# State in head rows, an early second batch, loads issued one by one, and 64-column tiles in a cross-attention and mixer kernel

## The chip, the core and the metric

The kernel runs on one core of one Trainium2 chip. The metric is device time in microseconds (us). Executions of one kernel mostly agree within a per cent or so. Each execution carries a state: "slow" here means over 1.5% above the fastest of the same kernel. A ratio is the mean time of one kernel's fast runs over that of the kernel before in the same rounds on the same chip, so it is not quite the ratio of the medians that stand beside it. Ratios come with a 95% interval.

## The reference

There are 8 batches and 8 heads. `x` has 512 tokens of 64 columns per head, `state` has 32. Both parts attend to each other; the joined 544 tokens of 512 columns then go through a mixer.

```python
scores  = scale * x @ state^T            # per batch and head: 512 x 32
xread   = softmax(scores)  @ state       # 512 x 64
scores2 = scale * state @ x^T            # 32 x 512
sread   = softmax(scores2) @ x           # 32 x 64
y = concat(xread, sread) on tokens, heads joined on columns     # 8 x 544 x 512
W_tok = scale * (y @ w_q) @ (y @ w_k)^T  # 544 x 544
out   = relu(W_tok @ y) @ w_out          # 8 x 544 x 512, float32
```

## The kernel before

The whole program is one list of tokens, `name.batch.engine`, and each token emits one step. The engine letter is `p` for POOL, `v` for DVE, `a` for ACT, `t` for TensorE. So the list fixes the order on every engine. Steps that matter here: `ixN` loads batch N of `x`; `stc` casts the state to bfloat16, `stt` transposes it, `ste` and `stf` evict it; `stbd` builds block-diagonal state; `xT` transposes `x`; `pt` and `exp` are scores; `A` normalises on POOL; `wq`, `wk`, `v`, `mix` and `fin` are the mixer.

```python
    st_f = const.tile([B * H, NS, D], FP, name="st_f")     # state: 64 rows (batch, head)
    nc.sync.dma_start(out=st_f, in_=state...)              # 512 KB, the first load of all
    for g in range(4):                                     # batch 0 of x, in float32
        eng = nc.sync if g % 2 == 0 else nc.scalar
        eng.dma_start(out=x_f0[:, 2 * g : 2 * g + 2], in_=xsrc(0, 2 * g, 2 * g + 2))
    ...
    def load(n, b, e):                                     # batches 1 to 7 and w_out:
        if n == "iwo":                                     # POOL's queue casts to bfloat16
            nc.gpsimd.dma_start(out=w_o, in_=moe_w_out.rearrange("(k p) e -> p k e", p=128))
        else:
            b = int(n[2:])
            nc.gpsimd.dma_start(out=x_bf[b], in_=xsrc(b, 0, H))
    ...
    def st_back(n, b, e):        # the transposed state is transposed back into head rows
    ...
```

In the list of before all of `ix1` to `ix7` and `iwo` are issued between 8.2 and 18.6 us. They stand in one queue, called the casting queue below.

The softmax here doesn't subtract the row's maximum and nothing guards it: scores larger than these inputs give would overflow.

## Time and profile before

| | before |
|---|---|
| median (range) | 95.72 us (95.07 to 96.07, 4 runs) |
| span of the profiled run | 93.4 us |
| TensorE busy | 85% |
| TensorE's waits for the state | 2.4 + 2.4 us |
| TensorE's last matmul to the end | about 5.6 us |

### The profile page before, as it was taken

What the parts mean: (1) busy time and instruction counts of PE and PEld (TensorE: products, weight loads), DVE (VectorE), ACT (ScalarE), POOL (GpSimd) and SP (SyncE); (2) the same over time, 40 slices, a digit from 0 to 9 for tenths busy, and PEclk for the clock granted to TensorE, in tenths of its full rate; (3) what the DMA queues carried; (4) which work ended last, traced back from release to release, by engine and by line L of the source; (5) the groups of instructions that cost most, each with busy time, mean ns of one, the idle gap of its engine ahead of it and who ended that gap; (6) DMA issues with size and microseconds to landing.
All of it is one profiled execution on the core that took longest, in us unless ns stands there. A gap on an engine that the chain in (4) does not pass through costs nothing.

```text
span 93.4 us, 3134 instructions
## 1 busy us (share of the span) xinstructions
PE 79.8 (85%) x1376; PEld 53.4 (57%) x1376; DVE 56.2 (60%) x109; ACT 53.6 (57%) x80; POOL 44.6 (48%) x58
## 2 busy tenths in 40 slices
PE   5908098998995999999999999999999999999500
PEld 3506086896864676888366547646668644444100
DVE  1026948589584959896496198965786487222500
ACT  2324746687894687359967647864054876444200
POOL 7307994894499989899500009339750000000000
PEclk9998555599999999999999999999999999999985
DMA  1998799999999915500032517806455004428990
GB/s 28 305 260 193 94 160 156 205 203 194 197 199 197 201 18 232 225 11 0 0 130 102 225 22 213 311 30 270 186 225 232 0 0 164 173 39 300 400 363 21
DMA packets 12933, 15.13 MB, mean 162 GB/s; under 512 B 1592, under 2 KB 10296, under 8 KB 12856
## 3 DMA queue, kind: packets, MB, share of 16 engines
q0 software_dynamic: 7808, 4.19, 33.2%
q1 hardware_dynamic: 4280, 9.70, 29.3%
q10 hardware_dynamic: 832, 1.05, 3.8%
q8 instruction: 10, 0.16, 0.7%
q14 instruction: 3, 0.02, 0.1%
HBM read 10.22 MB, written 8.91 MB: 205 GB/s over the span
## 4 chain that ended last, share of the span: by engine, by line
PE 76%; ACT 6%; DMA 6%; DVE 4%; issue 2%; DVEq 0%
PE fin_ps L538 30%; PE xT_ps L246 9%; DMA st_f<-in_state_dram 6%; PE pt_ps L264 5%; PE mix_ps L504 5%; PE at_ps L322 4%; PE srd_ps L335 3%; PE wq_ps L398 3%; PE wk_ps L436 3%; DVE stT L139 3%; ACT xT L137 2%; PE fins_ps L538 2%; PE srd_ps L348 2%; PE v_ps L468 2%; PE g_ps L452 2%
## 5 line engine op out<-in xcount | busy, mean ns | idle before, releaser
L538 PE MATMUL fin_ps<-w_o,rmix 128*128 128x512 bf16 x128 | 30.0, 379 | 0.0
L309 POOL TENSOR_TENSOR A<-E,rinv 128x1024 bf16<-128x1024 bf16 (+1 forms) x9 | 15.3, 1718 | 15.5 <-DVE rinv L303 15.5
L538 PEld LDWEIGHTS <-rmix 128*128 128x128 bf16 x128 | 11.6, 98 | 12.5 <-ACT rmix L143 0.3
L137 ACT COPY ost<-fin_ps 128x1024 f32<-128x1024 f32 (+1 forms) x10 | 9.3, 928 | 14.1 <-PE fin_ps L538 13.6
L139 DVE COPY ost<-fin_ps 128x1024 f32<-128x1024 f32 (+1 forms) x8 | 8.7, 1089 | 11.1 <-PE fin_ps L538 7.5
L280 ACT ACTIVATE E<-pt_ps 128x512 bf16<-128x512 f32 x16 | 9.6, 603 | 4.3 <-PE pt_ps L264 4.3
L372 POOL TENSOR_TENSOR sbd<-srn,mask 128x256 bf16<-128x256 bf16 x16 | 9.5, 612 | 4.4 <-DVE srn L362 4.1
L295 DVE TENSOR_REDUCE rsum<-E 128x16 f32<-128x512 bf16 x16 | 10.6, 672 | 1.1 <-ACT E L280 1.1
L246 PE MATMUL xT_ps<-ident,x_bf 128*128 128x128 bf16 x128 | 11.0, 238 | 0.1
L145 DVE TENSOR_SCALAR rmix<-mix_ps 128x1024 bf16<-128x1024 f32 x7 | 8.5, 1223 | 2.7 <-PE mix_ps L504 2.6
L137 ACT COPY xT<-xT_ps 128x1024 bf16<-128x1024 bf16 x9 | 9.1, 1020 | 1.5 <-PE xT_ps L246 1.5
L143 ACT ACTIVATE rmix<-mix_ps 128x1024 bf16<-128x1024 f32 x9 | 9.3, 1032 | 0.7 <-PE mix_ps L504 0.5
L213 POOL TENSOR_TENSOR stbd<-st_bf,mask 128x256 bf16<-128x256 bf16 x16 | 9.3, 614 | 0.0
L246 PEld LDWEIGHTS <-x_bf 128*128 128x128 bf16 x128 | 8.4, 106 | 1.0 <-issue 0.4
L264 PE MATMUL pt_ps<-stT,xT 128*128 128x64 bf16 x128 | 7.1, 203 | 0.5 <-DVE xT L139 0.4
L504 PE MATMUL mix_ps<-wq,V 64*128 64x256 bf16 x64 | 5.7, 272 | 1.2 <-issue 1.1
L152 POOL DMA_DIRECT2D x_bf<-in_x_dram x7 | 6.6, 944 | 0.0
L264 PEld LDWEIGHTS <-xT 128*128 128x128 bf16 x128 | 5.6, 105 | 1.6 <-DVE xT L139 0.5
L139 DVE COPY xT<-xT_ps 128x1024 bf16<-128x1024 bf16 x7 | 4.8, 686 | 2.2 <-PE xT_ps L246 2.0
L139 DVE COPY AT<-at_ps 128x1024 bf16<-128x1024 bf16 x7 | 4.8, 685 | 1.2 <-PE at_ps L322 1.2
L322 PE MATMUL at_ps<-ident,A 128*128 128x128 bf16 x64 | 5.0, 219 | 0.0
L504 PEld LDWEIGHTS <-V 64*128 64x128 bf16 x64 | 2.4, 94 | 3.8 <-issue 2.8
(76 smaller groups left out, 115.9 us busy)
## 6 DMA issues: line engine op xcount, KB each, us to landing
out_dram<-ost SPq DMA_DIRECT2D x14, 512.0 KB, 3.8
x_bf<-in_x_dram POOLq DMA_DIRECT2D x7, 512.0 KB, 13.4
out_dram<-ost SPq DMA_DIRECT2D x4, 256.0 KB, 2.1
st_f<-in_state_dram SPq DMA_DIRECT2D x1, 512.0 KB, 5.6
x_f<-in_x_dram ACTq DMA_DIRECT2D x2, 256.0 KB, 4.3
x_f<-in_x_dram SPq DMA_DIRECT2D x2, 256.0 KB, 6.3
w_o<-in_moe_w_out_dram POOLq DMA_DIRECT2D x1, 512.0 KB, 10.5
out_dram<-ost ACTq DMA_DIRECT2D x2, 256.0 KB, 3.9
```

Source lines behind the costliest of these rows:

```text
L137: nc.scalar.copy(out=out, in_=in_)
L139: nc.vector.tensor_copy(out=out, in_=in_)
L143: nc.scalar.activation(out=out, in_=in_, func=AF.Relu)
L213: nc.gpsimd.tensor_tensor(out=stbd[:, b, r], in0=st_bf[:, b, r : r + 1, :].to_broadcast((128, NP, D)), in1=mask[:, :, None].to_broadcast(( ...
L246: nc.tensor.transpose(out=ps[:, u, q, :], in_=x_bf[b][:, NP * r + q, 128 * u : 128 * u + 128], identity=ident,)
L264: nc.tensor.matmul(out=ps[:, 2 * u : 2 * u + 2, NS * q : NS * q + NS], lhsT=L[b][f"xTe{r}"][:, u, q, :], rhs=stT[:, b, :, NP * r + q, :], ...
L280: nc.scalar.activation(out=L[b]["E"][:, r].rearrange("p c q n -> p c (q n)"), in_=L[b][f"pt{r}"], func=AF.Exp, scale=float(scale),)
L295: nc.vector.reduce_sum(out=L[b]["rsum"][:, w], in_=L[b]["E"].rearrange("p r c q n -> p (r c q) n")[:, w], axis=AX.X,)
L309: eng.tensor_tensor(out=L[b]["A"].rearrange("p r c q n -> p (r c q) n")[:, w], in0=L[b]["E"].rearrange("p r c q n -> p (r c q) n")[:, w], ...
L372: nc.gpsimd.tensor_tensor(out=L[b]["sbd"][:, r], in0=L[b]["srn"][:, r : r + 1, :].to_broadcast((128, NP, D)), in1=mask[:, :, None].to_broa ...
L504: nc.tensor.matmul(out=ps[:, h, kk, :], lhsT=L[b]["V"][rows, 128 * k : 128 * k + 128], rhs=L[b]["wq"][rows, 0:SH], start=True, stop=True,)
L538: nc.tensor.matmul(out=ps, lhsT=lhs(k), rhs=w_o[:, k, :], start=(k == 0), stop=(k == KC - 1))
```

## The change

The intent is an earlier start and no state wait: load the state in the rows in which it is wanted, in three pieces (batch 0; 1 and 2; 3 to 7), with the last piece held back; issue `x1` early and `x4` to `x7` late, so that they don't crowd the queue; fill the early gaps with dummy matmuls that keep the clock up; and split some matmuls into two 64-column tiles.

```diff
-    st_f = const.tile([B * H, NS, D], FP, name="st_f")
+    st_f = const.tile([128, B, 2, D], FP, name="st_f")
+    gate = st_f[:, 3, 0, 0:1]
+    st_src = state.rearrange("b (r q) n d -> (q n) (b r) d", r=2)
+    def st_load(b0, b1):
+        nc.sync.dma_start(out=st_f[:, b0:b1], in_=st_src[:, 2 * b0 : 2 * b1])
+    st_load(0, 1)
     ... x0 in four loads
+    st_load(1, 3)
...
+    def fill(n, b, e):                         # b dummy matmuls of 512 columns
...
+    def mm(m, out, lhsT, rhs, **kw):
+        if m == "c":                           # two 64-column tiles
...
+    def st_gate(n, b, e):
+        nc.gpsimd.memset(gate, 0.0)            # the load below must wait for this write
+        st_load(3, B)                          # batches 3 to 7, 320 KB
...
-    def st_back / stb_ev                       # way back of the state: gone
...
+        if e == "b":                           # last output tile: half on DVE, half on ACT
```

In the list (cut):

```diff
-zst.0.p stc0.0.v ... ix1.0.p ... ix2.0.p ... iwo.0.p ... ix3.0.p ... ix4.0.p ... ix5.0.p ... ix6.0.p ... ix7.0.p
+zst.0.p ix1.0.p stc.0.v fill.1.t stt.0.c ... ix2.0.p ... fill.10.t ... iwo.0.p ... stbd.1.p ... stg.0.p
+... ix3.0.p ... stc.2.v ... v.0.c ... ix4.0.p ... fin3.0.c ix5.0.p ... xTe0.5.v ix6.0.p ... xT0.6.t ix7.0.p
```

## The prediction

> **What bounds the kernel now.** I read the page first (busy shares, then the 40 slices), then TensorE's waits, then the chain of work that ended last, and last a table of busy time per microsecond for the start. From the page, busy time and share by engine, then the slices:
>
> ```profile
> PE 79.8 (85%) x1376; PEld 53.4 (57%) x1376; DVE 56.2 (60%) x109; ACT 53.6 (57%) x80; POOL 44.6 (48%) x58
> ...
> PE   5908098998995999999999999999999999999500
> ...
> PEclk9998555599999999999999999999999999999985
> ```
>
> A slice is 93.4/40 = 2.33 us. TensorE is full from slice 8 (about 19 us) to slice 37, so the long middle is bound by TensorE's own stream. The losses are in front: holes in slices 0 to 12, and a half clock in slices 4 to 7. TensorE's waits, longest first:
>
> ```profile
> PE stT_ps L180 <- DVE st_in L139: 2.4, 1, 2.4
> PE stb_ps L201 <- ACT stT L137: 2.4, 1, 2.4
> PE mix_ps L504 <- issue: 1.1, 1, 1.1
> PE warm_ps L127 <- DVE mask L128: 1.1, 1, 1.1
> ```
>
> The two waits of 2.4 us are both about the state: first for its 512 KB load (issue to landing 5.6 us) and cast, then for four evictions of the transposed state, one after another. Per microsecond (busy time and count on PE, PEld, DVE, ACT, POOL, then granted clock, DMA share, GB/s):
>
> ```profile
> 8.00:9.00 1.00, 0.96 (x26) 0.68 (x20) 1.00 (x1) 0.00 (x0) 1.00 (x2) 0.82 0.82 138
> 9.00:10.00 1.00, 0.09 (x1) 0.00 (x0) 0.97 (x2) 0.86 (x1) 1.00 (x2) 0.50 0.08 18
> ...
> 18.00:19.00 1.00, 1.00 (x18) 1.00 (x16) 0.46 (x1) 0.33 (x1) 1.00 (x2) 0.56 1.24 208
> ```
>
> So the clock fell to half near 8.7 us and came back near 18.9. The chain (start, length, what) gives TensorE's prices:
>
> ```profile
> 39.36 0.34 PE v_ps L468 x2
> 39.69 0.22 PE v_ps L477 x4
> 39.91 0.22 PE v_ps L468 x2
> 40.13 0.22 PE v_ps L477 x4
> 40.35 0.22 PE wq_ps L398 x4
> ...
> 51.67 1.73 PE fin_ps L538 x8
> ...
> 72.65 1.09 ACT V L490 x2
> 73.74 0.01 issue
> 73.75 1.03 ACT rmix L143
> ...
> 87.77 0.59 ACT ost L137
> ```
>
> Eight 512-column matmuls take 1.73 us, 0.216 each. Two 512-column matmuls on 64-column tiles take 0.22 together, so they run side by side. The same pair right after full-array work costs 0.34. I compared all pieces of the chain after 20 us with columns/2.4 GHz plus 2.5 ns: the rest is 0.00 to 0.04 us in the same tile form and 0.10 to 0.12 (once or twice 0.15 to 0.17) where the form changes. I use 0.11 per change. At 72.65 TensorE's chain goes through ACT for 2.1 us. It ends at 87.77, and the copy, store and close take another 5.6.
>
> **What the Trainium skill says.** "TensorEngine Tiling (Array Packing)", Key Properties: changing the tiling mode drains TensorE, and tiles run independently; both agree with the 0.11 us and the paired 0.22 above. "TensorE: Matmul & The Clock Gate", Part 1: an idle window of about 3.4 us gives half clock, a busy one gives the full clock back, and the window runs freely. The trace agrees: two holes of 2.4 us, then ten microseconds at 0.50; and the first 16 matmuls of 256 columns start 0.21 us apart, which is 256/1.2 GHz, a cold start that the clock row does not show. The same page, Back-to-back issue gap, gives N/2.4 + 2.5 ns, 216 ns for 512 columns; measured 0.216. "DMA: Bandwidth & Descriptors", Specifications, asks for runs of at least 512 B for line rate. The new state load has 256-byte runs; no trace of before tests that.
>
> **The change, part by part.**
> *Dense work.* From the instruction lists I priced every matmul as above. Before: 63.3 us without dummies, with 61 form changes (6.7 us). After: 63.0 us and 57 changes (6.3). The state's way back (16 transposes, 0.23 us) goes, and the halved full matmuls run in pairs at the same price. So the 64-column tiles and the grouping are worth only about 0.4 us + 0.3 us. Their splitting cannot make the matmuls themselves cheaper.
> *Start.* Before, at 15.44 us (the first transposes of x1), 66.8 us of the stream were still to come. After, the same 66.7 us remain when it starts the transposes of x1's second half. I walk to that point with durations from before. Eight warm matmuls of 512 columns cold: 8 x 0.427 = 3.4, to 4.5 us. The first state piece is 64 KB; the earliest 256 KB load of before took 3.0 us, so it is there near 3.5 to 4, and its four transposes are done by 5.3. Ten dummies, mostly at full clock, to about 7.7. The x0 loads no longer stand behind 512 KB of state and should all be down by 5 to 6, POOL's cast included. xT0.0 0.45; ACT's eviction 1.02 to 9.1; scores near 9.2 and 9.6 (before: 13.25 and 14.24). ACT: a state eviction about 0.55, two exponentials 0.6 each, to 10.9. DVE's weight cast ends near 10.8; dummies fill, then sw and sums to 11.5. x1 is issued on POOL near 3.1 us; x1 needed 7.2 us before, so about 10.5. Start of the remaining 66.7: about 11.5, 3.9 us earlier than before.
> *The next ten microseconds.* DVE paces them, not TensorE: reductions 0.69, srn 0.46, xT 0.69, sw 0.68, AT 0.69 in a row put wq.0 at about 15.5 us with 63.9 us to come. v.0 comes near 19.7 with 60.3 to come, and mix1.0 waits for V on DVE (three state and reduction items ahead of it) until about 22.1 with 58.7 to come: 80.8 us if nothing stalls afterwards. The full clock saves what before lost between 15.4 and 18.9 (about 1.5 us), but eviction waits give some of it back.
> *x4 to x7.* POOL reaches the issue of x4 near 21.6 us. Before, eight loads took some 27 us, about 3.3 each; with 2 us of latency an isolated one is about 5.3, so x4 lands near 26.9 and is wanted near 26.0. x5 comes out similarly. I add 1.2 us for this once, not per load, as a late load moves everything behind it.
> *The end.* v.7 now has wk.6, fin1.3 and g.6 (1.4 us) between it and its mix, so the 2.1 us through ACT at 72.65 should be gone. My count of 80.8 includes that.
> *Tail.* The last output is halved over DVE and ACT, but the 512 KB store of batch 6 is issued after DVE's half on the same queue, about 1.4 us after TensorE ends instead of 0.4. It lands in 3.8 and the close takes 1.1: 6.3; less contention may make it 5.7. I take 6.0 against 5.6.
> *Sum.* 80.8 + 1.2 + 6.0 = 88.0 us of span, against 93.4: 5.4 less. From the median 95.5 that is 90.1; from the profiled run (95.16 less 93.4 is 1.8 outside the span) 89.8. I say 90.0.
>
> **Rivals.**
> *The loads become the bound.* Issuing x4 to x7 late gives up the long queue of before, in which x_bf landings took 7.2 to 17.0 us but always early enough: only 0.3 us of weight-load wait went to them. If an isolated load takes 7 us instead of 5.3, each of the four may cost up to 1.5 us: 93 to 95. For it: POOL works through its list in order and blocks of some 1.2 us stand before each issue. Against: no output stores before 34 us were in the way, and the loads alone get the engines.
> *Eviction becomes the bound early.* DVE was 8.4 of 10 us busy between 30 and 40, and after gives it more instructions than ACT (110 to 66 in the lists). If DVE paces the kernel up to 40 us, 2 us more: 92. For: my own walk waits for DVE three times before 22 us. Against: over the whole run DVE would be near 60 of 88 us.
> *The dummies overrun or the clock stays low.* 21 dummies of 0.216 are 4.5 us; if the clock is still half, the ten before xT0.0 take 4.3 and all comes 2 us later: 92. The free-running window makes this vary by run, like the 1 us spread of before.
> *The schedule is tight everywhere.* If loads and evictions fit exactly and the tail is 5.6, the end is 86.4 of span: 88.3.
>
> **Range and chances.** The gain rests on two seen losses (state wait, half clock), and it would take two bad rivals together to lose 4 of the 5.4 us. Range 88.2 to 92.4. Faster by over 2% (below 93.6): 0.95; within 2%: 0.04; slower: 0.01.
>
> **What would show it.** Right: clock at full without the half stretch from 9 to 19; first pt near 9.2; TensorE ending near 82; the 2.1 us of ACT near the end gone; form changes still 0.11. Wrong: a PEld or PE wait on x_bf above 1.5 us; a half-clock stretch beyond 8 us; first pt after 11; more than 6.5 us from TensorE's last matmul to the end; or halved fin groups of 0.216 per matmul instead of per pair.

## More of the kernel before

The prediction shows the busy row, the slices, the waits and the chain of this kernel. One more view matters afterwards, the DMA issues of the page. The last number of a line is the median from issue to landing in us.

```profile
x_bf<-in_x_dram POOLq DMA_DIRECT2D x7, 512.0 KB, 13.4
...
st_f<-in_state_dram SPq DMA_DIRECT2D x1, 512.0 KB, 5.6
```

A load of `x` took 13.4 us, but in a queue in which up to seven loads stood at once. The trace of before holds no load of `x` that ran alone. The state, issued first, landed in 5.6.

## The result

The prediction was wrong, in direction too. The changed kernel took 99.18 us in the median (98.69 to 99.82, 4 runs), against 95.72. The ratio is 1.0374 (1.0289 to 1.0458): slower by 3.7% where a gain of 6% was expected. The profiled run has a span of 97.5 us, against 93.4 before and 88.0 in the prediction's sum.

From the page of the changed kernel, the busy shares and the 40 slices (one slice is 97.5/40 = 2.44 us):

```profile
PE 83.0 (85%) x1419; PEld 53.6 (55%) x1429; DVE 59.9 (61%) x124; ACT 48.1 (49%) x71; POOL 44.1 (45%) x58
...
PE   5999799709999999579999999999999999999400
...
PEclk9999999995799999975999999999999999999975
```

The intended part came out: the first eight slices are well filled and at full clock. But there are two new losses, an empty slice 8 (from 19.5 us) and a dip in slices 16 and 17 (39 to 44 us), and a low clock follows each. TensorE's longest waits, as engine, tile and line, what ended the wait, us in total, times, longest:

```profile
PE stT_ps L217 <- DVE st_bf L144: 3.1, 1, 3.1
PE xT_ps L170 <- DMA x_bf<-in_x_dram: 1.8, 1, 1.8
```

The first is the third piece of the state, the second is the load of `x5`. The DMA issues of the page, which answer to the two lines of before:

```profile
x_bf<-in_x_dram POOLq DMA_DIRECT2D x7, 512.0 KB, 7.9
...
st_f<-in_state_dram SPq DMA_DIRECT2D x1, 320.0 KB, 11.9
```

The loads of `x` became shorter, as intended, but not short: the four that were issued one by one took 6.0, 7.2, 8.8 and 8.7 us, the last two overlapping each other. The state is now smaller and slower: 320 KB in 11.9 us. The chain of work that ended last (start, length, what) runs through both:

```profile
9.57 0.05 POOL st_f L192
9.62 0.02 issue
9.63 11.88 DMA st_f<-in_state_dram
21.51 0.03 issue
21.61 0.50 DVE st_bf L144
22.15 0.75 PE stT_ps L217 x12
...
36.97 0.69 POOL A L348
37.66 1.18 issue
38.84 1.75 POOL A L348
40.59 0.10 issue
40.69 8.79 DMA x_bf<-in_x_dram
49.48 0.05 issue
49.53 0.62 PE xT_ps L174 x8
```

At 9.57 POOL writes the gate element; only then is the state issued, and it lands at 21.51. DVE's cast of that piece stands in its list ahead of evictions that TensorE needs. DVE sat idle for 3.8 us until the landing, and between 20 and 22 us nothing but that cast ran on any engine. The second half of the lines is the load of `x6`: POOL comes to its issue only after two normalisations `A`, at 40.69, and the load takes 8.79. What this did to the clock is in the windows (us; busy time and count on PE, PEld, DVE, ACT, POOL; granted clock, DMA share, GB/s):

```profile
20.00:22.00 2.00, 0.00 (x0) 0.00 (x0) 0.40 (x1) 0.00 (x0) 0.00 (x0) 1.00 0.08 10
22.00:30.00 8.00, 7.83 (x188) 6.24 (x190) 6.58 (x17) 5.99 (x9) 5.92 (x10) 0.79 0.57 69
40.00:45.00 5.00, 3.22 (x52) 2.03 (x46) 1.92 (x6) 0.00 (x0) 4.84 (x7) 0.78 1.15 276
45.00:50.00 5.00, 4.62 (x87) 3.47 (x86) 3.38 (x6) 3.24 (x5) 0.00 (x0) 0.88 1.33 174
```

A mean clock of 0.79 over 8 us is 3.4 us at half clock (8 x 0.21/0.5), worth about 1.7 us of work; 40 to 50 us gives the same 3.4 us (5 x 0.22/0.5 + 5 x 0.12/0.5) and another 1.7. The clock records of this trace say the same: half clock from 22.31 to 25.72 and from 42.79 to 46.20 us. The busy row hides this: TensorE counts as 98% busy from 22 to 30 us, but part of it at half speed. The 1.7 us are worked out for the profiled run only. Its mean clock is 0.947; the other three runs have 0.964 to 0.967, about what one such stretch less would give (0.965), and their spans, 97.4, 98.0 and 96.9 us, are no shorter. So that a half-clock stretch costs its 1.7 us in every run isn't shown.

The gap between the predicted 88.0 us and the measured 97.5 us of span can be laid out by the landmarks of the prediction:

| landmark | predicted | measured | added since the one before |
|---|---|---|---|
| wq.0 starts | 15.5 | 16.4 | 0.9 |
| mix1.0 starts | 22.1 | 27.0 | 4.0 |
| TensorE's last matmul | 82.0 | 91.1 | 4.2 |
| end | 88.0 | 97.5 | 0.4 |

So two stretches cost 8.2 of the 9.5 us: the one with the state wait, and the one with the loads of `x5` and `x6`.

### The profile page after: what moved, and what is told of

It reads as the page before. It is cut to its first block, busy times and chain, and to the rows that moved or that the text cites. A ratio compares the mean times of both kernels' runs of the same rounds, so it can differ in the third digit from the quotient of the medians.

```text
span 97.5 us, 3245 instructions
## 1 busy us (share of the span) xinstructions
PE 83.0 (85%) x1419; PEld 53.6 (55%) x1429; DVE 59.9 (61%) x124; ACT 48.1 (49%) x71; POOL 44.1 (45%) x58
## 4 chain that ended last, share of the span: by engine, by line
PE 52%; DMA 26%; DVE 6%; POOL 4%; issue 3%; ACT 1%; SPq 1%; DVEq 1%; POOLq 0%
PE fin_ps L163 21%; DMA st_f<-in_state_dram 12%; DMA x_bf<-in_x_dram 9%; DMA x_f<-in_x_dram 5%; PE xT_ps L174 4%; PE mix_ps L543 3%; DVE rsum L334 3%; POOL A L348 3%; PE pt_ps L163 2%; PE g_ps L163 2%; PE v_ps L507 2%; PE fin_ps L161 2%; PE fins_ps L163 2%; PE wk_ps L163 2%; PE v_ps L516 2%
## 5 line engine op out<-in xcount | busy, mean ns | idle before, releaser
L163 PE MATMUL fin_ps<-w_o,rmix 128*128 128x512 bf16 x99 | 24.5, 380 | 0.6 <-issue 0.2
L144 DVE COPY ost<-fin_ps 128x1024 f32<-128x1024 f32 (+2 forms) x10 | 10.3, 1035 | 6.6 <-PE fin_ps L163 3.8
L142 ACT COPY ost<-fin_ps 128x1024 f32<-128x1024 f32 (+2 forms) x9 | 8.0, 893 | 11.3 <-PE fin_ps L163 7.6
L144 DVE COPY xT<-xT_ps 128x1024 bf16<-128x1024 bf16 x11 | 7.6, 689 | 3.4 <-PE xT_ps L170 2.1
L142 ACT COPY AT<-at_ps 128x1024 bf16<-128x1024 bf16 x5 | 5.1, 1015 | 7.3 <-PE at_ps L170 6.9
L174 PE MATMUL xT_ps<-ident,x_bf 128*128 128x128 bf16 x104 | 8.0, 220 | 0.2 <-DMA x_bf<-in_x_dram 0.2
L142 ACT COPY xT<-xT_ps 128x1024 bf16<-128x1024 bf16 x5 | 5.1, 1011 | 3.9 <-PE xT_ps L174 3.9
L161 PE MATMUL fin_ps<-w_o,rmix 128*64 128x512 bf16 x40 | 6.2, 439 | 0.0
L155 PE MATMUL fill_ps<-zero 128*128 128x512 bf16 x20 | 6.1, 394 | 0.1
L142 ACT COPY stT<-stT_ps 64x512 bf16<-64x512 bf16 (+2 forms) x4 | 2.3, 582 | 6.4 <-PE stT_ps L217 3.8
## 6 DMA issues: line engine op xcount, KB each, us to landing
st_f<-in_state_dram SPq DMA_DIRECT2D x1, 320.0 KB, 11.9
```

The source lines that it names most:

```text
L142: nc.scalar.copy(out=out, in_=in_)
L144: nc.vector.tensor_copy(out=out, in_=in_)
L161: nc.tensor.matmul(out=out[64 * h : 64 * h + 64], lhsT=lh, rhs=rhs, **kw)
L163: nc.tensor.matmul(out=out, lhsT=lhsT, rhs=rhs, **kw)
L174: nc.tensor.transpose(out=out, in_=in_, identity=ident)
```

## The experiments

Three theories went in. Theory 1: the late third piece of the state is the cause. Theory 2: the loads issued one by one are. Theory 3 came after the first results: once both are mended, TensorE's own instruction fetches become late, because they share the DMA engines with the casting queue.

### The state's third piece issued at once

```diff
             nc.sync.dma_start(out=w_f[64 * r : 64 * r + 64, :, t, :], in_=wsrc[t][r])
+    st_load(3, B)
...
- ... exp0.0.a stg.0.p wc.0.v ...
+ ... exp0.0.a wc.0.v ...
```

> The last 320 KB of the state are issued right after the weights (near 5.5 us) instead of behind POOL's gate at 9.63. If the late issue is what costs (theory 1), they land some 4 us earlier, near 15 to 17.5 us, TensorE's 3.1 us wait for the state cast and the clock drop behind it go, and the time falls from 99.2 to 94 to 96. If the state load is slow because it shares the DMA engines with the queue of x1, x2, w_out and x3 (rival), it still lands after 18.5 us, x1 lands later than 10.9, and the time stays above 97.5.

Measured: ratio 0.9949 (0.9835 to 1.0063). Four runs, 95.2 and 95.49 fast, 98.94 and 100.31 slow. The state landed in 7.0 us and its wait is gone. Why half of the runs were slow isn't settled. In the profiled run, a fast one, mix1.0 starts at 22.5 us instead of 27.0, without a hole in it, but three loads of `x` are each late by up to 2.0 us:

```profile
22.54 0.61 PE L544 MATMUL mix_ps<-wq,V 64*128 64x256 bf16 x8
...
PE xT_ps L175 <- DMA x_bf<-in_x_dram: 4.0, 3, 2.0
```

By the ratios the gate was worth 4.2 of 103.7 parts, about 4 us. But the waits for `x` grew from 2.0 (1.8 and 0.2) to 4.0 us: part of the time saved in front is lost again at the loads. Theory 2 isn't dead.

### The loads together again, the state still held back

```diff
- ... ix4.0.p ... ix5.0.p ... ix6.0.p ... ix7.0.p ...     (their late places)
+ ... ix3.0.p ix4.0.p ix5.0.p ix6.0.p ix7.0.p ...
```

> x4 to x7 are issued right behind x3 as in the kernel before; all else as in the changed kernel. If the one-by-one issue costs by itself (theory 2), the 1.8 us wait for x5 and the half clock behind it go: 99.2 minus about 3 to 4, so 95 to 96.5, with the 3.1 us state wait still there. If the late x5 is only a consequence of the late state (POOL waits 2.3 us for it), the saving here is still the x5 wait, but the fuller queue may slow the state load further, to a net of less than 2 us: above 97.

Measured: 95.65 us, ratio 0.9973 (0.9893 to 1.0053). No wait for `x` is left. The state landed in 11.5 us, as late as in the changed kernel, yet its wait was 1.5 us, because TensorE had lost 1.9 us before it at an `A` of POOL. The time is in the range of the first branch of the expectation, but not by its sum: mix1.0 starts at 26.5, little earlier than in the changed kernel, and the gain comes after it. So undoing either half recovers nearly the whole loss, and the two can't add up.

### Both at once

The two diffs above together.

> Both edits. If the two waits are separate and add up, 99.2 minus 5 minus 3.5, so about 90 to 92, which is what was predicted for the change. If one wait only hides the other, no faster than the better of the two single edits by more than 1 us. If neither is the cause, 97 or more.

Measured: 94.64 us, ratio 0.9883 (0.9792 to 0.9974), span 92.8. That is 1.2% below before, and 4.7 us of span below the changed kernel (97.5 - 92.8). The expectation's 90 to 92 was missed: the two savings don't add up, and the gain over the better of the single edits is under 1 us. Still, with both undone the kernel isn't slower than before, so theories 1 and 2 together account for the reversal. The state's load took 12.6 us here, but it was issued some 4 us earlier and nobody waited for it. The largest losses that are left, against the 88.0 predicted, are two holes that the timeline puts down to "issue" (start, length, instructions, in brackets the idle time before and what ended it).

```profile
25.28 0.50 PE L544 MATMUL mix_ps<-wq,V 64*128 64x256 bf16 x6 [1.28 <-issue]
31.20 0.24 PE L249 MATMUL sw_ps<-w_qk,stT 64*32 64x128 bf16 x6 [1.38 <-issue]
```

The profile shows nothing that they waited for. The same kind of hole stood in the kernel before, in the wait `PE mix_ps L504 <- issue` of 1.1 us that the prediction shows but doesn't explain.

### The state through the casting queue

```diff
     def st_gate(n, b, e):
-        nc.gpsimd.memset(gate, 0.0)
-        st_load(3, B)
+        nc.gpsimd.dma_start(out=st_bf[:, 3:B], in_=st_src[:, 6 : 2 * B])
...
- ... ix1.0.p ... stg.0.p ... stc.2.v ...
+ ... ix1.0.p stg.0.p ...
```

> The last 320 KB of the state go through the casting queue, straight behind x1, so that they need not share with what is queued behind them, and no cast on DVE. If order in the queues is what makes the state late, it lands near 13 us, x2 near 15 to 16, no state wait on TensorE, time 94 to 96. If 256-byte runs are slow by themselves, the queue behind it is held up: x2 after 17 us, and the time stays above 97.

Measured: 97.16 us, but three of four runs were slow; the one fast run took 94.62, so no ratio is given. The state wait is gone, the waits for `x` are 4.8 us. On time this run is inconclusive. On the waits it repeats the first experiment, though the profile is of a slow run (97.02 us).

### Each late load one place earlier

Here the state is not held back, and `x4` is issued after `A1.0`, with `x5`, `x6` and `x7` in the old places of `x4`, `x5` and `x6`. The second kernel does the same with the state in the casting queue.

```diff
- ... A1.0.p ... ix4.0.p ... ix5.0.p ... ix6.0.p ... ix7.0.p ...
+ ... A1.0.p ix4.0.p ... ix5.0.p ... ix6.0.p ... ix7.0.p ...     (5 to 7 in the old places of 4 to 6)
```

> State not gated (as in e1), and each of x4 to x7 issued one place earlier in POOL's list: still apart from one another, so that the casting queue drains in between. If the one-by-one issue fails only because each load is issued too late (theory 2), the waits for x (4.0 us in e1) go; if a full queue starves TensorE's instruction fetch (theory 3: both 1.3 us holes of e3 open at instruction rows 704 and 960, 256 rows apart, with no wait in them), these holes are here below 0.5 us. Time 92.5 to 94, against 94.6 with all loads together. If theory 3 is wrong, the holes at these rows stay and the time is 94.5 or more.

Measured: 94.12 us, ratio 0.9844 (0.9754 to 0.9935), span 92.5, clock 0.993. No wait for `x` and none for the state, but holes put down to "issue" of 1.5, 1.4 and 0.7 us. For theory 3 this was a miss: it had said that the queue would drain between the loads and the holes fall below 0.5 us. The packet records of the trace show that the queue hardly drained. It moved packets from 10.73 to 23.24 us without a pause and again from 23.68 to 27.63.

> As e5_shifted, but the state's last 320 KB come through the casting queue behind x1 (as in e4). In e4 no state wait was left, only 4.8 us of waits for x. If those are only the late issue, they go here too: 92 to 93.5. If the state in front of x2 delays x2 and x3 in the queue, 1 us or more of waits for x2 or x3 stay and the time is 94 or more.

Measured: 94.18 us, ratio 0.984 (0.9737 to 0.9942): the same, and neither branch of the expectation. No wait for `x` is left, but a wait of 2.0 us for the weight cast `w_qk` and 2.0 us of issue holes (0.44, 1.10 and 0.43).

### The end as before

The first takes the kernel with both at once, the second the one with shifted loads and the state in the casting queue. Both restore the end of before: the last tile whole on ACT, and the store of batch 6 ahead of it.

```diff
- ... os0.6.s fix0.7.t oe1.6.v oc0.7.b os1.6.s
+ ... os0.6.s oe1.6.v os1.6.s fix0.7.t oc0.7.a
```

> As e3_both (94.6), with the end as in the kernel before: the last output tile is copied whole on ACT, and the copy and store of its neighbour come ahead of it in the order. In e3 and in the changed kernel 7.1 us pass from TensorE's last matmul to the end, 5.6 in the kernel before. If the halved last tile and the store behind it are the reason, 5.6 to 6.0 here and a time of 93.1 to 93.6; if the end is slow because of stores already under way, no change: 94.3 to 95.

Measured: 94.37 us, ratio 0.9854 (0.9767 to 0.9941). Against the third experiment, whose loads it has, 0.3 us in the medians, in another round: no difference that the intervals show. This is the "no change" branch of the expectation. Its 7.1 us from TensorE's last matmul to the end is a misreading: the traces give 6.3 in the changed kernel and in the third experiment, 6.2 here and 5.65 in before. So the halved last tile isn't where the time went, and what makes the end 0.6 us longer than before isn't settled.

> e6 with the end of e7. If all causes are found and add up: 90.5 to 92.5, the time that was predicted for the change itself. If one is still missing, above 93.

Measured: 95.35 us with two slow runs of four; fast runs 0.9836 (0.9713 to 0.996). That is the branch "one is still missing": no gain over its sister with the new end (0.984).

### Full tiles, to move the list under the holes

If a hole belongs to an instruction, it stays with it. If it belongs to a place in TensorE's list, it moves to other instructions when the list gets shorter. Putting the 64-column tiles of `fin`, `xT`, `at` and `srT` back to full ones takes 176 rows out of the list. The base is the kernel with shifted loads. The expectation is about the price of the tiles; this test of the holes was read from the run afterwards. The forecast for the holes stands with the next experiment.

```diff
- ... xT0.3.c ... fin3.0.c ... at.3.c ... srT.4.c ...
+ ... xT0.3.t ... fin3.0.t ... at.3.t ... srT.4.t ...      (and all others of the four)
```

> e5_shifted with the 64-column tiles of output groups, late transposes and srT back to full tiles (same order). The list then has 66 changes of tile form instead of 57: 9 x 0.11 = 1.0 us more on TensorE, all in the dense part, so 95.0 against 94.1. If the halved matmuls cost something themselves (rival: they are the reason that the change was slow), the time falls below 93.5 instead. TensorE's list is also 176 rows shorter, so instruction fetches fall elsewhere late in the run, which could take back some tenths.

Measured: 94.05 us, ratio of the fast runs 0.9815 (0.9762 to 0.9869), so neither the 95.0 nor the "below 93.5" of the expectation. The holes moved to other instructions:

```profile
24.28 0.21 PE L564 MATMUL mixs_ps<-wq,V 64*128 64x32 bf16 x2 [0.97 <-issue]
29.93 0.51 PE L175 MATMUL xT_ps<-ident,x_bf 128*128 128x128 bf16 x6 [1.24 <-issue]
```

A row is one instruction of TensorE's list, a weight load or a matmul. The holes open at rows 704 and 960 of its own list (to within two rows), as they do in before and in the second, the third and the shifted experiments above; 704 and 960 are 256 rows apart. The trace also has a DMA queue of kind "instruction", with 0.16 MB in 10 packets in before, 16 KB each: one page of instructions. Laid beside TensorE's rows (worked out from the trace's records, us):

```
                      row 704 runs   last fetch before it    hole    row 704 to next fetch
before                    22.95        20.63 to 21.52         0.3            3.7
shifted loads             24.02        21.57 to 22.51         1.5            3.6
both mended               25.28        22.79 to 23.68         1.3            3.7
changed kernel            26.90        19.87 to 20.76         none           2.5
                      row 960 runs   last fetch before it    hole
before                    29.14        26.63 to 27.52         1.1
shifted loads             29.94        27.57 to 28.65         1.4
both mended               31.20        28.93 to 29.82         1.4
changed kernel            31.65        29.35 to 30.24         0.1
```

"Shifted loads" and "both mended" are the runs told above. Wherever there is a hole, the row runs 1.3 to 1.6 us after the fetch before it ended. In each line with a last column, the next fetch begins only after TensorE has passed row 704. It begins 3.6 to 3.7 us after, where the casting queue is full, but 0.2 to 0.3 us after in before at 36.4 and 40.6 us, when the queue was empty. The 256 rows from 704 to 960 took 5.9 us with shifted loads.

That the queue is what delays the fetch, the first and the third experiment show: their lists for TensorE are the same, and they differ only in when `x4` to `x7` are issued. In the first experiment, the queue's packets end at 20.14 us and begin again at 24.12. The fetches after rows 448 and 704 began 1.0 and 0.4 us after those rows, and neither row 704 nor row 960 has a hole (before row 960 TensorE also waited 2.0 us for `x`). In the third the queue was full throughout. The two fetches began 3.5 and 3.7 us after, with 1428 packets of the queue in the second of these stretches, and the holes are 1.3 and 1.4 us. So theory 3 is shown, as to what the holes are and as to the queue.

"Runtime: NRT & Kernel Launch", section "Instruction fetch mechanics", of the Trainium skill states that each engine fetches its instructions in 16 KiB blocks of 256 by its own DMA queue, and that the cost of crossing a boundary is "mostly hidden". The block size agrees. The hiding doesn't hold here: the holes above last up to 1.5 us each.

The same run answers another question: with full tiles the ratio is 0.9815, with 64-column tiles it was 0.9844, and the intervals overlap. No value of the 64-column tiles is shown, and none of their price.

### Without the dummy matmuls

```diff
- ... fill.1.t stt.0.c ... fill.10.t xT0.0.t ... fill.5.t sw.0.r ...
+ ... stt.0.c ... xT0.0.t ... sw.0.r ...                   (all 21; on shifted loads)
```

> e5_shifted without the 21 dummy matmuls in the gaps (the 8 warm ones stay). Theory 3 (instruction fetch): TensorE's rows move up by 42, so the holes must open at rows 704 and 960 of the new list, which are inside a wk group and a pt group, and no longer inside mix and sw. Clock: without dummies TensorE idles from about 5 to 7.5 us and half clock may follow as in the kernel before; then 1 to 3 us slower (95 to 97). If the dummies do nothing for the clock, 93.5 to 94.5.

Measured: 93.56 us (fast runs 92.97, 93.76, 93.35), ratio 0.9751 (0.9689 to 0.9812). This is the lowest ratio here, 2.5% below before, though the intervals of its neighbours overlap it. It is a miss of the expectation twice: no 1 to 3 us were lost, and no holes opened at rows 704 and 960. Its slices and its waits:

```profile
PE   4939429998999999988999999999999999999200
...
PEclk9999995899999999999999999999999999999985
```

```profile
PE sw_ps L248 <- DVE w_qk L144: 3.0, 1, 3.0
PE xT_ps L174 <- POOL x_bf L187: 1.4, 1, 1.4
```

The clock is granted as high without dummies, except in slices 6 and 7. TensorE waits 4.4 us in front for casts, where the others ran dummies, but the holes at rows 704 and 960 are gone: their next pages were asked for 0.3 and 0.1 us after the crossings, not 3.6. The packet records show why. The queue moved nothing from 24.90 us, when `x4` was through, to 25.78, when `x5` began, and row 704 came at 25.20. `x5` was through at 29.58, and row 960 came at 29.57.

> e10_no_fill (93.4 in its fast runs) with full tiles. 9 more changes of tile form cost 1.0 us if nothing else moves: 94.3. In e9 this did not show, which I put down to smaller fetch holes (2.2 instead of 3.6 us); in e10 there were no fetch holes to save, so here the 1.0 us must show. If the time stays at 93.4, the price of a change is hidden and the 64-column tiles are worth nothing.

With full tiles as well: 93.95 us with one slow run of four, ratio of the fast runs 0.9774 (0.9672 to 0.9875), the same within its interval. Here the hole at row 960 is back, and long:

```profile
PE pt_ps L163 <- issue: 1.9, 1, 1.9
```

Here the queue paused from 23.59 to 25.04 us and row 704 came at 24.76, 0.3 us before the pause ended. The fetch began at 28.53, when the queue's next burst was nearly through (28.85). So leaving out the dummies doesn't remove the holes. A few tenths of a us decide whether a crossing falls into a pause of the queue, and that no hole opened in the run above was luck.

> e10_no_fill with the four weight loads on ACT's queue right behind x0, about 1 us earlier. In e10 TensorE waits 3.0 us for the weights' cast. If that wait is on the path, 1 us earlier weights give 92.4 to 92.9. If the weights land no earlier because the DMA engines are busy with x0 and x1, no change: 93.2 to 93.8.

The weights' loads were moved to ACT's queue (`nc.scalar.dma_start(out=w_f ...)`) to shorten the wait for `w_qk`, which fell to 1.0 us. Measured: 95.12 us with two slow runs of four, ratio of the fast runs 0.981 (0.969 to 0.9929): no gain shown, as ACT's late cast of `x0` took its place with 2.1 us.

> The changed kernel without its 21 dummies, all else as it is. If the dummies hold the clock and pay for themselves, slower than 99.2 by 1 us or more. If they only take up TensorE's list and time, 98 to 99.2: the state wait at 22 us is set by the DMA and hides what the dummies gain or lose before it.

The changed kernel itself without its dummies: 101.9 us, two runs slow; fast runs 100.71 and 100.07, ratio 1.0514 (1.0406 to 1.0623). That is 1.2 us above the changed kernel in the means of the fast runs (100.4 - 99.2, of different rounds), but the intervals of the two ratios overlap (1.0289 to 1.0458), so a gain by the dummies isn't shown. The profile puts the difference elsewhere than in front: `x5`, issued at 34.8 us as in the changed kernel, landed 2.5 us later, and TensorE waited.

```profile
PE xT_ps L169 <- DMA x_bf<-in_x_dram: 4.7, 1, 4.7
```

Whether the missing dummies made that load late is open. No run here shows a worth of the dummies.

### Two measurements of the queue

> e5_shifted with w_out loaded as float32 on the plain queue into the buffer that x0's cast has freed, and cast by POOL after its first sbd. It takes one of five loads off the casting queue between 8 and 27 us. If the busy casting queue is what delays TensorE's instruction fetch (theory 3), the hole at row 960 goes and that at row 704 shrinks: 92 to 93.2. If the fetch is delayed by any DMA traffic or for another reason, the holes stay at 1.4 us each: 94 or more.

`w_out` was loaded in float32 on the plain queue and cast on POOL, to shorten the casting queue. Measured: 101.32 us and above in three slow runs, 97.8 in the fast one. A miss: the plain 1 MB load took 15.1 us beside the casting queue, and TensorE waited 5.0 us for POOL (both in the profile of a slow run). As a test of theory 3 it is void: TensorE came to row 704 only at 30.2 us. Rows 704 and 960 have no hole there, but a hole of 3.0 us stands at row 1472, 512 rows further.

> A measurement, not a faster kernel: as the changed kernel, but x2, w_out and x3 are issued only after A1 on POOL (near 13.5 us), so that the gated 320 KB of state (256-byte runs) share the DMA engines with the rest of x1 alone. If sharing with the casting queue made it take 11.9 us, it lands in 3 to 5 us here. If its short runs did, it still takes over 8 us.

Here `ix2`, `iwo` and `ix3` of the changed kernel are issued only after `A1.0`, so that the held-back state has the DMA engines nearly to itself. The kernel is made for the measurement and takes 106.96 us in its one run.

```profile
st_f<-in_state_dram SPq DMA_DIRECT2D x1, 320.0 KB, 4.4
```

The same 320 KB in the same runs of 256 bytes took 4.4 us nearly alone and 11.9 beside the casting queue. So the length of the runs, which the prediction had noted as the risk of this load, isn't enough to make it late; the sharing is needed. Whether longer runs would fare better while sharing, no run tests. This is one run, of unknown state.

## Why the prediction was wrong

**The step that failed first** is in its walk "The next ten microseconds". It moves from `wq.0` at "about 15.5" to mix1.0 at "about 22.1" without a word on when the third piece of the state lands (it names "three state and reduction items" on DVE, not the load behind them). The prediction priced the first piece, 64 KB, and never the 320 KB that POOL lets go at 9.63 us and that DVE casts ahead of the evictions that TensorE waits for. In its place the runs showed 11.9 us from issue to landing, a wait of 3.1 us and 3.4 us at half clock after it. That stretch is 4.0 us longer than predicted. Letting the load go at once removed the wait, and mix1.0 came at 22.5 (first experiment), near the walk's 22.1. In part that nearness is luck: the transposes of `x1` came 1.4 us later than in the walk. Giving the load the engines nearly alone cut it to 4.4 us.

**The second failed step** is the term for the loads: "an isolated one is about 5.3" and "I add 1.2 us for this once". The mechanism was named, the size was off. The loads took 6.0 to 8.8 us, and POOL came to the issue of `x6` only at 40.69 us. From mix1.0 to TensorE's last matmul the walk had 58.7 + 1.2 = 59.9 us, and the profiled run took 64.1. The kernels without waits for `x` (second and third experiment, shifted loads) took 60.0 to 60.3 for the same stretch with their instruction holes taken off. So the late loads cost about 4 us, not 1.2: waits of 1.8 and 0.2, about 1.7 through the half clock, and about 0.5 in small gaps put down to "issue". And the count of 58.7 was 1.3 to 1.6 too low, which is open. In the trace of before the eight loads took 25.7 us (8.20 to 33.90), not 27, so 3.2 each. The 2 us of latency held: 1.6 from the issue of `x4` to its first packet and 0.35 after the last. Its packets took 4.0 us (26.09 to 30.06). The later loads also ran beside output stores, and `x6` and `x7` overlapped each other.

**The rival that came closest** was "The loads become the bound": it had the load at 7 us, but stopped at "93 to 95". The argument against it, that no output stores would be in the way before 34 us, was beside the point, since only `x4` was issued before that. Its own sign had been set right: a wait on `x_bf` above 1.5 us, and the profile has 1.8. No rival had the state's load in it.

**What held.** The start, roughly: full clock to 22 us, the first `pt` at 9.56 us against 9.2, the transposes of `x1` at 12.6 against 11.5. A form change of TensorE's tiles still costs 0.11 us, and two halved `fin` matmuls still run as a pair in 0.216. The 2.1 us through ACT near the end is gone. "So the 64-column tiles and the grouping are worth only about 0.4 us + 0.3 us": no run shows more than that. The tail took 6.3 us against 6.0; DVE's half and ACT's half of the last tile ran one after the other (90.37 to 91.93 and 91.96 to 92.33), and the end as before shortened the tail by 0.1.

**What stood between the plan and 88 even with both mended.** With shifted loads no wait for state or `x` is left, and TensorE still ended at 86.15 us instead of 82.0. Since mix1.0 started at 22.2, as in the walk, and no wait for a load was left, 80.9 would have been due. The instruction holes of 1.5, 1.4 and 0.7 us are 3.6 of these 5.2, and the count that was too low is the rest. The holes were in the profile of before, as one wait of 1.1 us put down to "issue", and I passed over it. Of the expected 5.4 us of span, the version with shifted loads got 0.9 (93.4 to 92.5), and without dummies 2.2 (91.2).

**A loss that the record doesn't bear out.** The prediction rests its gain on "two seen losses (state wait, half clock)". The kernel before also ran without the long half-clock stretch. In the profiled run 10.2 us at half clock in front, and the fall at the end, make a mean of 0.93; nine of its 27 fast runs listed with the experiments have a mean of 0.97 to 0.99, which leaves no room for ten such microseconds. Their spans are 93.4 to 94.5 us (mean 94.0), those of the other 18, at 0.92 to 0.94, 92.9 to 94.7 (mean 93.4). So the full clock in front didn't make that kernel faster. What held it back instead isn't known, as no such run was profiled. One reading of the clock is off too: the prediction says that the trace agrees with an idle window of 3.4 us, but the clock fell at 8.63 us, after one hole of 2.4 us (4.65 to 7.08) and before the second. In the changed kernel a hole of 1.8 us was followed by half clock, and in the first experiment one of 2.0 us was not.

**What stays open:** why the dense stream took 1.3 to 1.6 us more than counted; what the half clock costs; and why half the runs with the state let go at once were slow.

## What to carry to other kernels

Price every load that a change moves, the last piece as well as the first: when it is issued, what shares the DMA engines with it, and what stands behind it in the list of the engine that handles it. A load's time in a full queue says little about its time alone, and issuing loads one by one trades queueing for the time at which the issuing engine gets to them. A wait put down to "issue" on a long instruction list is worth locating in the list: here such holes came 256 rows apart and were instruction fetches, late behind a queue of loads.

## What the Trainium skill lacked or had wrong

- "Runtime: NRT & Kernel Launch", section "Instruction fetch mechanics": a block boundary is called mostly hidden; in the fast runs profiled here TensorE stood up to 1.9 us at a single boundary, after a fetch that came late behind the casting queue.
- "DMA: Bandwidth & Descriptors", section "Anatomy of one DMA — SWDGE (gpsimd) path": the fit of about 2.0 us plus bytes at 436 GB/s gives 3.2 us for the 512 KB written and 4.4 us for the 1 MB read (estimates from the page); a casting load of `x` took 5.8 to 5.9 us when no other stood in its queue (`x6` and `x7` without dummies and with full tiles), and 6.0 to 8.8 us in the changed kernel.
- No page gives the time of a load on the plain queue beside a busy casting queue: 11.9 us against 4.4 us nearly alone for the same 320 KB.
- "TensorEngine Tiling (Array Packing)", Key Properties, tells of a drain at a change of form but gives no price: 0.11 us here.
